# Four half pieces of expert 0's weights: the subtraction of the split on VectorE instead of GpSimd, in units 16 to 19

## The chip, the cores and the metric

The kernel runs on one core of a Trainium2 chip. The metric is the device time of one execution in microseconds (us). An engine runs its own instructions in the order in which they were written; engines wait for each other by semaphores.

## The reference

Local and global attention, then a mixture of experts (MoE), in float32. Eight batches of eight heads hold 512 local and 32 global positions of width 64; a local query sees the global keys and the local ones at most 32 positions away:

```python
out_g = softmax(scale * q_g @ k_all.T) @ v_all
out_l = softmax(concat(scale * q_l @ k_g.T, where(|i - j| <= 32, scale * q_l @ k_l.T, -1e9))) @ concat(v_g, v_l)
x = concat(out_g, out_l) as rows of 512               # 4608 tokens
keep = x @ w_skip > 0
e = argmax(x[keep] @ w_gate)                          # one of 8 experts
out[keep] = x[keep] + gate * relu(x[keep] @ w1[e]) @ w2[e]
```

The MoE multiplies with weights and activations that are each split into a high and a low part: `hi` is the value cast to the matmul type float32r, and `lo = value - hi`. Three matmuls (hi by hi, hi by lo, lo by hi) stand for one.

## The kernel before

**Attention** runs in 32 units, numbered u. A unit is two heads of one batch, four units a batch. It is a software pipeline of three: in iteration u the names `cur`, `prev` and `old` are units u, u-1 and u-2. The list `ORDER` (L758) gives the order of the steps in an iteration, and with manual scheduling this is the order of each engine's queue. The steps that matter here:

- `cur.scores 0/1` (TensorE, L380) and `cur.probs 0` to `probs 3` (L393, L398): for each two windows VectorE adds the mask and finds the extreme, and ScalarE takes the exponential with its sum. The first such VectorE instruction of a unit reads the mask `m_first`; it marks the unit's start below. There are six of eight window instructions ahead of the step `split_mid`, the last two (`probs 3`) behind it.
- `cur.normal 0/1` (VectorE, L430, L431) invert the sums; `cur.scale 0/1` (GpSimd, L435) multiply the probabilities by them. `prev.turn_g 0/1` (VectorE, L511) read what they leave.
- `prev.scale_g` (GpSimd, L468), in odd iterations only, scales the global queries' probabilities; `prev.turn_pg` (TensorE, L492, L493) transposes them and `prev.turned_pg` (ScalarE L501, VectorE L504) copies them out.
- `old.gather_g 0`, `old.leave 0` (VectorE, L567, L560), `cur.window_min` (VectorE, L420, even units), `cur.probs_g` (VectorE L452, ScalarE L457, even units), `prev.turned 0` (VectorE, L483).
- `sends` (GpSimd, L691): two indirect DMAs a unit that write finished rows of the expert lists to DRAM. They stand ahead of `cur.scale 1` in GpSimd's queue.

**The split of expert 0's weights** is done during attention. Eight pieces of 128x1024 are loaded ahead, and each is split in two halves of 128x512, one half a unit from unit 4 to unit 19. A half is a cast on ScalarE (L188) that writes the high part, and a subtraction (L189) that reads the loaded piece and that high part, both in SBUF, and writes the low part. Up to unit 16 the step is `split`, the last of the iteration; from unit 17 it is `split_mid`, between `prev.scale_g` and `old.values 1`. The result is first read by the MoE, after the 32 units. Later experts' weights are split on VectorE, whole pieces at a time, through the same function.

**The MoE** runs the eight experts one after the other, with the next expert's weights loaded and split meanwhile.

Of the kernel before, what the change touches and what calls it, by code (L numbers as in the profile page):

```python
# [44 lines left out]
def kernel(  # L45
# [12 lines left out]
    nc = tc.nc  # L58
# [42 lines left out]
    def index(es, g):  # L101
        nc.vector.tensor_copy(six[:, es, g], lt[:, es, g, :, 0])
# [14 lines left out]
    def gather(xg, gidx, nrow=NT):  # L117
        for t in range(NSUB):
            ins = nc.gpsimd.indirect_dma_start(  # L119
                out=xg[:, t, :], out_offset=None, in_=out[0:nrow, :],  # L120
                in_offset=bass.IndirectOffsetOnAxis(ap=gidx[:, t:t + 1], axis=0),
                bounds_check=nrow - 1, oob_is_err=False,
            )
            apart(ins, "gathers", "scatters")
# [3 lines left out]
    def tick(n=1):  # L128
        for _ in range(n):
            if stages:  # L130
                stages.pop(0)()

    def send_some(n):
        for _ in range(n):
            if sends:
                sends.pop(0)()
# [54 lines left out]
    weights = {0: Weights(0, w1a, v1a, w2a)}  # L191
# [9 lines left out]
    def turn_x(xg, i, nt=NSUB):  # L201
        xh, xl = xs[i]
        for t in range(nt):
            pt = ps_t("xt")
            for c in range(NC):
                nc.tensor.transpose(  # L206
                    pt[:, c * P:(c + 1) * P], xg[:, t, c * P:(c + 1) * P], ident
                )
            p3 = pt.rearrange("p (c n) -> p c n", n=P)
            ts_ = slice(t * P, (t + 1) * P)  # L210
            step = NC if nt > 1 else NC // 2
            for c in range(0, NC, step):
                nc.scalar.copy(xh[:, c:c + step, ts_], p3[:, c:c + step])  # L213
            nc.vector.tensor_sub(xl[:, :, ts_], p3, xh[:, :, ts_].bitcast(F32))  # L214
        return xh, xl
# [4 lines left out]
    with ExitStack() as actx:  # L220
# [55 lines left out]
        def consts_pool():  # L276
            nc.gpsimd.memset(xfirst, 0.0)
            nc.gpsimd.affine_select(
                out=tri, in_=ones, pattern=[[1, P]], compare_op=ALU.is_gt,
                fill=0.0, base=0, channel_multiplier=-1,  # L280
            )
            nc.gpsimd.iota(ids_i, pattern=[[S, B], [P, 5]], base=SG, channel_multiplier=1)
            for hf in range(2):
                for bb in range(4):
                    nc.gpsimd.iota(
                        ids_i[bb * 32:(bb + 1) * 32, 4 * hf + 3, 4:5], pattern=[[0, 1]],
                        base=(4 * hf + bb) * S, channel_multiplier=1,
                    )
            nc.gpsimd.iota(tmp[:, 0, :], pattern=[[-1, E]], base=E, channel_multiplier=0)
            nc.gpsimd.iota(tmp[:, 1, :], pattern=[[CAP, E]], base=0, channel_multiplier=0)  # L290
# [25 lines left out]
        def load_qg(b):  # L316
            for h in range(2):
                hp = slice(h * D, (h + 1) * D)
                nc.sync.dma_start(
                    qgs[b % 2][hp, :, h * 32:(h + 1) * 32],  # L320
                    qgT[b, :, hp, :].rearrange("p d q -> d p q"),
                )

        def load_vg(b):

            for h in range(2):
                for o in range(2):
                    r = (2 * h + o) * 32
                    nc.sync.dma_start(
                        vgs[b % 2][r:r + 32, :, o, :], vgl[b].rearrange("p s d -> s p d")  # L330
                    )

        def load_pair(u):
            b, p = divmod(u, NP)
            nc.sync.dma_start(ks[u % NQ].rearrange("d r o m -> d (r o m)"), kT[b, p])
            n = SL // 2 if u == 0 else SL
            for i in range(0, SL, n):
                nc.sync.dma_start(qs[u % NQ][:, i:i + n], qT[b, p, :, i:i + n])

        def load_v(u):  # L340
            b, p = divmod(u, NP)
            nc.sync.dma_start(vw[u % NV].rearrange("k i d -> k (i d)"), v[b, p])
# [430 lines left out]
        with tc.manual_schedule(engines=engines):  # L773
# [19 lines left out]
            for u in range(NU + 2):  # L793
                cur = pair(u) if u < NU else None

                nth = iter(range(8))

                def seam():
                    tick(1 if u < NU - 4 else 2)
                    if u >= NU or u == NU - 2 and next(nth) in (0, 1, 4, 5):  # L800
                        send_some(1)

                def late_rows():
                    for b, k in LATE_ROWS.get(u, ()):
                        batch_rows(b, k)
                    if u == NU - 1:
                        for k in range(5):
                            batch_rows(B - 1, k, (0,))

                def loads_g():  # L810
                    if u < NU and u % NP == 2 and u // NP + 1 < B:
                        load_qg(u // NP + 1)
                        load_vg(u // NP + 1)

                def loads_pair():
                    if u + 2 < NU:
                        load_pair(u + 2)

                def loads_v():
                    if 2 <= u + 1 < NU:  # L820
                        load_v(u + 1)

                def early_rows():
                    bp, kp = divmod(u - 6, NP)
                    if 0 <= bp < B - 3:
                        batch_rows(bp, kp)
                        if kp == 3 and bp % 4 == 3:
                            batch_rows(bp, 4)

                def first_x():  # L830
                    if u == NU - 1:
                        index(first, 0)
                        gather(xfirst, six[:, 0, 0, :], (B - 2) * S)

                def last_x():
                    if u == NU:
                        x2.append(turn_x(xfirst, 0))

                def setup():
                    if u == 0:  # L840
                        consts_pool()

                def setup_late():
                    if u == 1:
                        clear_batch(1)
                        consts_late()

                def split():
                    if u == NU - 1:
                        for _ in range(2):  # L850
                            load_piece(1)
                    if u == 3:
                        weights[0].load()
                    if 4 <= u <= 16:
                        split_one()

                def split_mid():
                    if u > 16:
                        split_one()

                def split_one():
                    if u % 2 == 0:
                        weights[0].load()
                    weights[0].split(nc.gpsimd, 2)

                def after():
                    if u == NU - 2:
                        send_some(len(sends))
                        slots(first, 0)
                    if u == NU - 1:  # L870
                        tick(len(stages))

                def last_sends():
                    if u == NU - 1:
                        send_some(len(sends))

                def some_sends():
                    if u < NU - 1:
                        send_some(2 if u < NU - 3 else 4)

                loose = dict(
                    loads_g=loads_g, loads_pair=loads_pair, loads_v=loads_v,
                    rows=early_rows, late_rows=late_rows, first_x=first_x, setup=setup,
                    setup_late=setup_late, split=split, after=after, seam=seam, sends=some_sends,
                    last_sends=last_sends, split_mid=split_mid, last_x=last_x,
                )
                for step in ORDER:
                    name, _, arg = step.partition(" ")
                    if name in loose:
                        loose[name]()  # L890
                        continue
                    who, name = name.split(".")
                    it = dict(cur=cur, prev=prev, old=old)[who]
                    if it is None or name in PAIR and it.u % 2:
                        continue
                    getattr(it, name)(*([int(arg)] if arg else []))
                prev, old = cur, prev
# [269 lines left out]
```

## Time and profile before

| | |
|---|---|
| median of 3 runs | 474.61 us (474.32, 474.61, 477.75) |
| the profiled execution | 478.56 us, of which its span (first to last instruction) is 476.8 us |
| busy over the span | TensorE 92%, VectorE 64%, ScalarE 60%, GpSimd 49% |
| attention, the last unit's start | 202.85 us |
| the 16 subtractions of expert 0's split | GpSimd, 35.1 to 125.4 us, 20.4 us in all |

In the rows below PE is TensorE, PEld its weight load, DVE VectorE, ACT ScalarE, POOL GpSimd. Times are us from the span's start, unless a column says ns. The shares of the whole span average attention and MoE, which have different limits, so the rows are taken from the units that the change touches. A timeline row is: start, duration, engine, line, operation, output<-inputs with shapes, count, and in brackets the engine's idle time before it with what ended it.

### The profile page before, as it was taken

How to read it: one execution, taken by the hardware profiler on the slowest of the kernel's cores; microseconds unless marked ns; L12 is line 12 of the kernel's file. 1: busy time of each engine (PE TensorE's matmuls, PEld its weight loads, DVE VectorE, ACT ScalarE, POOL GpSimd, SP SyncE). 2: the span in 40 equal slices, each digit the busy share in tenths (PEclk: the TensorE clock that was granted, in tenths of full speed). 3: DMA queues.
4: the chain of work that ended last, by engine and by line, in shares of the span. 5: the costliest groups of instructions: out<-in, count | busy, mean ns of one | idle time of the engine just before them, and what ended most of it. 6: DMA issues, size and time to landing. Idle time of an engine off the chain costs nothing. (4 is left out here: it accounts for less than half of the span.)

```text
span 476.8 us, 13622 instructions
## 1 busy us (share of the span) xinstructions
PE 438.9 (92%) x4962; PEld 370.8 (78%) x4962; DVE 307.1 (64%) x1239; ACT 283.8 (60%) x867; POOL 231.9 (49%) x238
## 2 busy tenths in 40 slices
PE   7799999998899999788979999999999999899991
PEld 3687878786788776667958898979879898698980
DVE  7798888997779889864533184848417574166510
ACT  5599999998889998664412072728126272254500
POOL 7557777789966878873442050505005150032300
PEclk9799999999999999999989999999999999999996
DMA  7998898989898896412637047575604858037000
GB/s 250 301 346 282 282 312 310 316 286 305 248 314 256 218 294 155 128 46 90 112 60 284 24 143 281 164 267 172 256 1 136 309 153 305 3 104 257 27 18 17
DMA packets 50593, 93.32 MB, mean 196 GB/s; under 512 B 15644, under 2 KB 19996, under 8 KB 50496
## 3 DMA queue, kind: packets, MB, share of 16 engines
q1 hardware_dynamic: 44384, 80.78, 53.1%
q0 software_dynamic: 6112, 11.30, 7.1%
q8 instruction: 55, 0.90, 0.8%
q14 instruction: 42, 0.34, 0.3%
HBM read 82.91 MB, written 14.67 MB: 205 GB/s over the span
## 5 line engine op out<-in xcount | busy, mean ns | idle before, releaser
L398 ACT ACTIVATE prob<-prob,nmx 128x160 f32<-128x160 f32 x256 | 106.7, 423 | 16.4 <-DVE nmx L393 16.1
L435 POOL TENSOR_TENSOR prob<-prob,inv 128x640 f32<-128x640 f32 x64 | 80.5, 1260 | 33.8 <-DVE inv L431 15.0
L1008 POOL DMA_INDIRECT out_dram<-yo,six x12 | 12.2, 1016 | 125.4 <-DVE yo L1007 107.9
L931 ACT ACTIVATE hh<-ph 128x256 fp32r<-128x256 f32 x72 | 27.7, 384 | 66.3 <-PE ph L926 60.4
L942 PE MATMUL py<-w2h,hh 128*128 128x512 f32 x144 | 57.0, 396 | 0.0
L942 PE MATMUL py<-w2h,hlw 128*128 128x512 f32 x144 | 56.4, 391 | 0.0
L942 PE MATMUL py<-w2l,hh 128*128 128x512 f32 x144 | 56.3, 391 | 0.0
L380 PE MATMUL pss<-ks,qs 64*64 64x160 f32 x1024 | 52.5, 309 | 3.5 <-DMA qs<-in_qT_dram 1.7
L532 PEld LDWEIGHTS pv<-ptT,vw 128*64 128x64 f32 x1024 | 41.4, 138 | 18.4 <-issue 9.9
L398 ACT ACTIVATION_READ_ACCUMULATOR prob<-prob,nmx 128x1 f32 x256 | 49.4, 193 | 0.0
L532 PE MATMUL pv<-ptT,vw 128*64 128x64 f32 (+1 forms) x1024 | 47.8, 240 | 0.8 <-DVE ptT L483 0.2
L926 PE MATMUL ph<-xh,w1h 128*128 128x256 f32 x288 | 46.0, 282 | 2.3 <-DVE xl L214 1.1
L926 PE MATMUL ph<-xh,w1l 128*128 128x256 f32 x288 | 45.3, 279 | 0.0
L926 PE MATMUL ph<-xl,w1h 128*128 128x256 f32 x288 | 45.3, 279 | 0.0
L380 PEld LDWEIGHTS pss<-ks,qs 64*64 64x64 f32 x1024 | 35.3, 135 | 11.3 <-issue 7.3
L932 DVE SCALAR_TENSOR_TENSOR hlw<-ph,hh 128x256 fp32r<-128x256 f32 x72 | 30.0, 418 | 20.2 <-ACT hh L931 19.4
L213 ACT CAST xh<-xt 128x512 fp32r<-128x512 f32 (+1 forms) x22 | 11.2, 550 | 52.9 <-PE xt L206 52.9
L926 PEld LDWEIGHTS ph<-xh,w1h 128*128 128x128 f32 x288 | 38.8, 188 | 4.7 <-issue 3.2
L691 POOL DMA_INDIRECT lst<-dat,slu x34 | 34.6, 1017 | 15.0 <-issue 6.3
L476 PE MATMUL pst<-ident,prob 128*128 128x128 f32 x256 | 39.7, 281 | 0.0
L926 PEld LDWEIGHTS ph<-xl,w1h 128*128 128x128 f32 x288 | 38.9, 189 | 0.0
L926 PEld LDWEIGHTS ph<-xh,w1l 128*128 128x128 f32 x288 | 38.7, 188 | 0.0
(179 smaller groups left out, 972.8 us busy)
## 6 DMA issues: line engine op xcount, KB each, us to landing
raw<-in_w_dram SPq DMA_DIRECT2D x58, 512.0 KB, 6.6
vw<-in_v_dram SPq DMA_DIRECT2D x32, 512.0 KB, 6.3
ks<-in_kT_dram SPq DMA_DIRECT2D x32, 400.0 KB, 5.1
out_dram<-xr SPq DMA_DIRECT2D x32, 256.0 KB, 4.5
qs<-in_qT_dram SPq DMA_DIRECT2D x31, 256.0 KB, 4.9
raw<-in_w_dram POOLq DMA_DIRECT2D x6, 512.0 KB, 8.0
vgs<-in_vgl_dram SPq DMA_DIRECT2D x32, 64.0 KB, 5.4
lst<-dat,slu POOLq DMA_INDIRECT x34, 4.5
```

The lines of the kernel that those rows point to most:

```text
L213: nc.scalar.copy(xh[:, c:c + step, ts_], p3[:, c:c + step])
L380: nc.tensor.matmul(banks[odd][head(h ^ odd), j * W:(j + 1) * W], q[head(h), w * QB:(w + 1) * QB], window(k[head(h)], w), start=True, stop= ...
L398: nc.scalar.activation(pt[:, i, :], pt[:, i, :], AF.Exp, bias=nmx[:, i:i + 1], scale=-1.0, accum_out=sums[:, i, 0:1],)
L435: nc.gpsimd.tensor_mul(pt[:, sl, :], pt[:, sl, :], inv[:, sl].unsqueeze(2).to_broadcast([P, 4, W]),)
L476: nc.tensor.transpose(pst[:, i * P:(i + 1) * P], pt[:, 4 * hf + i, 0:KW], ident)
L532: nc.tensor.matmul(pv[head(h), j * 96:j * 96 + n], vv[:, w, head(h)], ptT[:, w, h ^ odd, 0:n], start=False, stop=j == 3, skip_group_check= ...
L691: ins = nc.gpsimd.indirect_dma_start(out=lst, out_offset=bass.IndirectOffsetOnAxis(ap=slu[:, t:t + 1], axis=0), in_=dat[:, bs[j], t - 4 * ...
L926: nc.tensor.matmul(ph[:, 0:GRP], hl[a][:, c, f * P:(f + 1) * P], bb[:, c, :], start=i == 0, stop=i == 3 * NC - 1,)
L931: nc.scalar.activation(hh[:, f, :], ph[:, 0:GRP], AF.Relu)
L932: nc.vector.scalar_tensor_tensor(hlw[:, f, :], ph[:, 0:GRP], 0.0, hh[:, f, :].bitcast(F32), ALU.max, ALU.subtract,)
L942: nc.tensor.matmul(py, a[:, f, ts_], hl[bb][:, f, :], start=f == 0 and i == 0, stop=f == NF - 1 and i == 2,)
L1008: ins = nc.gpsimd.indirect_dma_start(out=out, out_offset=bass.IndirectOffsetOnAxis(ap=sidx, axis=0), in_=yo, in_offset=None, bounds_check= ...
```

## The change

The first sixteen halves were subtracted by GpSimd. Now the halves of units 4 to 15 still are, and those of units 16, 17, 18 and 19 go to VectorE. The place in the order of steps, the casts on ScalarE and the loads are the same.

```diff
                 def split_one():
                     if u % 2 == 0:
                         weights[0].load()
-                    weights[0].split(nc.gpsimd, 2)
+                    weights[0].split(nc.gpsimd if u < 16 else nc.vector, 2)
```

`Weights.split` (L182), which it calls, is unchanged:

```python
                nc.scalar.copy(hi, raw)
                eng.tensor_sub(lo, raw, hi.bitcast(F32))
```

## Rows read from the trace of the kernel before

**Rows 1.** First line of the profile page.

```profile
span 476.8 us, 13622 instructions
```

**Rows 2.** Stages: units 17 to 20, cut at each unit's first m_first instruction.

```profile
core 0: us, PE busy (x) PEld busy (x) DVE busy (x) ACT busy (x) POOL busy (x), PEclk, DMA share, GB/s
106.57:114.47 7.90, 6.42 (x131) 5.55 (x121) 5.23 (x32) 6.85 (x26) 7.42 (x8) 1.00 1.03 305
114.47:120.80 6.33, 6.33 (x112) 4.38 (x108) 5.26 (x32) 5.94 (x23) 5.76 (x6) 1.00 1.14 303
120.80:128.15 7.35, 5.57 (x117) 4.85 (x109) 4.81 (x30) 6.19 (x24) 6.86 (x7) 1.00 0.70 190
128.15:133.71 5.56, 5.56 (x111) 4.46 (x104) 5.01 (x32) 5.11 (x21) 4.92 (x5) 1.00 1.00 348
```

**Rows 3.** Waits, 106.4 to 128 us: waiter <- releaser: total us, times, longest.

```profile
PE psgT L492 <- POOL probg L468: 3.3, 2, 1.8
DVE pgT L511 <- POOL prob L435: 2.4, 5, 0.5
```

**Rows 4.** Groups by line: forms, count | busy us, mean ns.

```profile
L189 DVE TENSOR_TENSOR w2l<-raw,w2h 128x1024 fp32r<-128x1024 f32 x28 | 34.1, 1217 | 3.6 <-ACT w2h L188 3.6
...
L214 DVE TENSOR_TENSOR xl<-xt,xh 128x512 fp32r<-128x512 f32 x20 | 13.2, 687 | 22.9 <-ACT xh L213 22.9
...
L189 POOL TENSOR_TENSOR w2l<-raw,w2h 128x512 fp32r<-128x512 f32 x8 | 10.2, 1281 | 0.2
```

**Rows 5.** Timeline of VectorE, units 16 to 20.

```profile
106.35 0.30 DVE L511 STREAM_TRANSPOSE pgT<-prob 128x128 f32<-128x128 f32 x1
...
108.38 0.29 DVE L567 TENSOR_REDUCE xTg<-pv 128x32 f32<-128x128 f32 x1
...
115.91 0.22 DVE L420 CUSTOM_DVE_ANT_1 smg<-pss,zero 128x64 f32<-128x64 f32 x1
...
116.94 0.29 DVE L393 CUSTOM_DVE_ANT_0 prob<-pss,m_odd 128x160 f32<-128x160 f32 x1
...
122.48 0.28 DVE L567 TENSOR_REDUCE xTg<-pv 128x32 f32<-128x128 f32 x1
...
131.65 0.31 DVE L511 STREAM_TRANSPOSE pgT<-prob 128x128 f32<-128x128 f32 x1 [0.48 <-POOL prob L435]
```

**Rows 6.** Timeline of ScalarE, units 16 to 19.

```profile
106.64 0.61 ACT L188 CAST w2h<-raw 128x512 fp32r<-128x512 f32 x1
...
107.62 0.44 ACT L398 ACTIVATE prob<-prob,nmx 128x160 f32<-128x160 f32 x1
...
110.11 0.61 ACT L188 CAST w2h<-raw 128x512 fp32r<-128x512 f32 x1
...
118.12 0.43 ACT L398 ACTIVATE prob<-prob,nmx 128x160 f32<-128x160 f32 x1
...
121.19 0.43 ACT L398 ACTIVATE prob<-prob,nmx 128x160 f32<-128x160 f32 x1
```

**Rows 7.** Timeline of GpSimd, end of unit 16.

```profile
107.07 0.98 POOL L691 DMA_INDIRECT lst<-dat,slu  x1 [0.30 <-DVE nmx L393]
108.06 1.28 POOL L435 TENSOR_TENSOR prob<-prob,inv 128x640 f32<-128x640 f32 x1
```

**Rows 8.** One line's instructions: count: ns min/median/max, first and last start.

```profile
L671 DVE TENSOR_TENSOR oh<-mx,first x5: 202/873/1833, 92.4 to 225.1; 128x64 f32<-128x64 f32 x2, 128x72 f32<-128x72 f32 x1, 128x32 f32<-128x32 f32 x1, 128x40 f32<-128x40 f32 x1
```

**Rows 9.** Timeline of both engines, 143.9 to 145.3 us.

```profile
143.94 1.25 POOL L435 TENSOR_TENSOR prob<-prob,inv 128x640 f32<-128x640 f32 x1 [1.65 <-DVE inv L431]
...
144.41 0.87 DVE L671 TENSOR_TENSOR oh<-mx,first 128x72 f32<-128x72 f32 x1
```

**Rows 10.** Timeline of both engines, 198.4 to 200.3 us.

```profile
198.46 1.83 DVE L671 TENSOR_TENSOR oh<-mx,first 128x32 f32<-128x32 f32 x1
...
198.97 1.27 POOL L435 TENSOR_TENSOR prob<-prob,inv 128x640 f32<-128x640 f32 x1
```

## The prediction

> **What bounds the kernel now.** I forecast against the profiled execution, 478.56 us with a span of 476.8 us [rows 1]. The three runs have their median at 474.61 us, 4.0 us lower, so I work out a difference in us and add it to the median. Changes below 1% (4.7 us) can't be told from no change here.
>
> The first view is the table of stages, cut where a unit starts, at its first VectorE instruction on the scores [rows 2]. The whole-span shares on the page put GpSimd at half busy, which is an average with the MoE, where it does little. In unit 17 it is busy 7.42 of 7.90 us, in unit 18 5.76 of 6.33, in unit 19 6.86 of 7.35: over 90% each time, while VectorE is busy 5.23, 5.26 and 4.81 us. Unit 20, without a subtraction, has GpSimd at 4.92 of 5.56 us. So three of the four changed places lie where GpSimd sets the pace.
>
> The second view, the waits in these units, says the same from the other side [rows 3]: TensorE waits 3.3 us, twice, for the scaled global probabilities, and VectorE 2.4 us, five times, for the scaled ones. Read so, the change takes work off the bound. What the two views don't show is where a subtraction on VectorE would have to stand, and that decides my forecast.
>
> **What is removed.** Four instructions of 1.28 us on GpSimd [rows 4], 5.1 us in all. All of it is on the path of units 17 to 19 at most; I count the gain not by itself but in the unit lengths below, which are worked out as if GpSimd were never late.
>
> **What is added: four subtractions on VectorE.** This form, 128x512 with both inputs in SBUF, isn't in the trace. The same line with 1024 columns takes 1.217 us, and a 512-column subtraction with one input in PSUM 0.687 us [rows 4]. I take 0.69 us, the row of the same size; its bounds are half the long one, 0.61 us, and the whole long one, 1.22 us. The casts on ScalarE, the loads and SP's queue keep their places; the four loaded pieces come free at about the same time, and nothing else asks for their buffers before the last unit.
>
> **What is moved: a wait for ScalarE into the middle of VectorE's queue.** The subtraction needs the cast ahead of it. GpSimd came to its subtractions long after the casts; VectorE runs ahead of ScalarE and comes too early. Everything behind it on VectorE, which also feeds ScalarE's next exponentials, waits with it.
>
> *Unit 16.* The cast runs from 106.64 to 107.25 [rows 6]. In VectorE's queue the subtraction stands right ahead of the transpose that started at 106.35 [rows 5]. Starting 0.03 after the cast and taking 0.69 us, it ends at 107.97. Unit 17 therefore starts later by 107.97 - 106.35 = **1.62 us**.
>
> *The cast within a unit.* The first exponential comes 0.39 us after the unit's start when ScalarE isn't behind (unit 19: 121.19 against 120.80 [rows 2, 6]). Six exponentials stand ahead of the cast and took 110.11 - 107.62 = 2.49 us in unit 17; the cast takes 0.61 [rows 6]. So its result is there 0.39 + 2.49 + 0.61 = 3.49 us after the unit's start. VectorE reaches that place after its six score instructions: in unit 17 at 108.38 - 106.57 = 1.81 us, in unit 18 at 115.91 - 114.47 = 1.44 us, in unit 19 at 122.48 - 120.80 = 1.68 us [rows 2, 5]. The forced idle times are 1.68, 2.05 and 1.81 us.
>
> *Unit 17.* VectorE's own work 5.23, the subtraction 0.69 and the idle time 1.68 make 7.60 us against 7.90: **-0.30 us**. The GpSimd waits that it had are gone, and the new wait takes their place almost exactly.
>
> *Unit 18.* 5.26 + 0.69 + 2.05 = 8.00 us against 6.33: **+1.67 us**. VectorE's idle time before was 6.33 - 5.26 = 1.07 us, all that GpSimd's lateness can have cost here.
>
> *Unit 19.* ScalarE starts it somewhat late. In unit 18 the subtraction ends at 3.49 + 0.69 = 4.18 us; from L420 to the next score instruction VectorE needs 116.94 - 115.91 = 1.03 us [rows 5], and I add 0.37 until ScalarE has its result (the 0.39 above less one hop): 5.58. From there to the next unit's first exponential ScalarE needs 121.19 - 118.12 = 3.07 us without a pause [rows 6], so 8.65 us after unit 18's start, which is 0.65 after unit 19's instead of 0.39. The idle time is then 1.81 + 0.26 = 2.07 us, and the unit 4.81 + 0.69 + 2.07 = 7.57 us against 7.35: **+0.22 us**.
>
> *Unit 20.* GpSimd's backlog is gone, so the wait of 0.48 us at 131.65 [rows 5] disappears: **-0.48 us**.
>
> The sum is 1.62 - 0.30 + 1.67 + 0.22 - 0.48 = **+2.7 us**. Attention goes on in the same order, and the MoE begins when its last lists are written, so I carry the whole of it to the end: 474.61 + 2.7 = **477.3 us**, 0.6% slower. With the subtraction at 0.61 us the sum is 0.3 us less, at 1.22 us 2.1 us more (4 x 0.53).
>
> **Two engines at SBUF.** VectorE's L671 takes two SBUF inputs and 0.20 us at its shortest, but 1.83 at its longest [rows 8]. At 144.41 it took 0.87 us: GpSimd's multiplication had begun at 143.94 and ended at 145.19, and L671 ended 0.09 after that [rows 9]. So such a VectorE instruction waits for a multiplication of GpSimd that is under way. In units 17 to 19 as I have laid them out, GpSimd has finished or not begun one when the subtraction is issued, within 0.2 us in unit 19. In unit 16 the subtraction is issued at 107.28 and would end at 107.97, before the multiplication of 108.06 [rows 7].
>
> The Trainium skill, "SBUF — State Buffer", section "Who interferes with whom", says that a VectorE instruction with two SBUF inputs contends with a GpSimd instruction that reads SBUF, and that whoever issues first has the shared port for the whole instruction. The trace agrees where GpSimd was first (held to 0.09 us past the multiplication's end [rows 9]). By that rule unit 16's subtraction, issued first, is not held, and the sum stays +2.7 us.
>
> Another row points the other way: at 198.46 L671 began 0.51 us *before* the multiplication of 198.97, should have been done in 0.20 us, and yet ended at 200.29, 0.05 us after that multiplication's end at 200.24 [rows 8, 10]. Unit 16 has the same order, a send and then the multiplication [rows 7].
>
> **The rivals.**
> - *Held in unit 16.* The subtraction behaves as at 198.46 and waits for the end of the multiplication, 108.06 + 1.28 = 109.34. It starts 109.34 - 107.28 = 2.06 us later, with everything behind it: +4.8 us, 479.4 us. For it speaks the one row with the same order; against it that its start was 0.51 us ahead of the multiplication, here 0.78 us. Chance 0.30.
> - *Relief wins* (the other side). VectorE doesn't lose time at the casts, because ScalarE, also freed of its waits, brings them before VectorE needs them. Then the waits of rows 3 go, 3.3 + 2.4 us, and 4 x 0.69 us is paid: -2.9 us, 471.7 us. It decides for this where the cast's result is there less than about 1.7 us after the unit's start; six exponentials alone need 2.49. Chance 0.10.
> - *Absorbed.* The loss is there in unit 20 and is made up by waits in the twelve units behind, 0 us, 474.6 us. Nothing in rows 2 shows a resource with an own timetable; a transfer could be one. Chance 0.12.
> - *Forecast as summed*, 0.48.
>
> **How the numbers follow.** The likeliest case gives 477.3 us; its own range, with 0.61 to 1.22 us for the subtraction, is 477.0 to 479.4. The range 474.0 to 480.4 takes in the absorbed case, with 0.6 us for the runs' own spread below it, and the held one with 1 us for a longer subtraction, and leaves out the relief case. Slower by over 1% (above 479.4): half of the held case, 0.15, and 0.07 of the likeliest with a long subtraction, 0.22. Faster by over 1% (below 469.9): only a relief beyond its price, 0.03. The rest, 0.75, is within 1%.
>
> **What would show it.** Right: in units 16 to 19 VectorE has a wait for the cast (L188) ahead of L189, near 0.9, 1.7, 2.0 and 2.1 us, with L189 at 0.69 us each; ScalarE idles 1 us or more ahead of the last two exponentials of units 17 to 19; unit 18 takes about 8.0 us and the others about what they did; GpSimd drops below 85% and nobody waits for it. A first L189 of 2.7 us instead of 0.69 is the held case. Wrong: unit 20 starting no later than before, or units 21 to 31 getting shorter than they were by more than half a us in all.

## The result: 0.55% slower, and the profile after

The changed kernel takes 478.15 us in the median of 21 runs, the kernel before 475.66 us in 21 runs beside it. The ratio is 1.0055, with a 95% interval of [1.0039, 1.0071], so the change costs 2.6 us (1.9 to 3.4). The forecast was +2.7 us. (The two profiled executions, 478.57 us after and 478.56 before, don't show it: they are single ones. Between the start of unit 15 and the start of unit 31 they differ by 110.85 - 107.49 = 3.4 us; unit 16 begins at 101.20 us before and 100.10 after, and the MoE differs again behind. I therefore compare lengths of units.)

Units 17 to 20 after the change, in the columns of [rows 2]:

```profile
107.58:114.91 7.33, 5.33 (x71) 4.43 (x71) 5.44 (x33) 5.41 (x22) 4.39 (x4) 0.85 1.04 284
114.91:122.53 7.62, 7.62 (x128) 5.49 (x124) 5.65 (x32) 6.00 (x22) 4.62 (x5) 0.92 0.94 233
122.53:130.37 7.84, 6.33 (x118) 4.95 (x111) 5.24 (x32) 6.32 (x25) 5.59 (x6) 1.00 0.93 312
130.37:135.78 5.41, 5.41 (x100) 4.41 (x104) 5.10 (x32) 5.28 (x21) 4.04 (x5) 1.00 0.82 157
```

Against [rows 2], unit 17 is 0.57 us shorter, unit 18 1.29 longer, unit 19 0.49 longer, unit 20 0.15 shorter. GpSimd is busy for 4.39 of 7.33 us, 4.62 of 7.62 and 5.59 of 7.84: it no longer sets the pace, and still the four units together are 1.06 us longer, behind a unit 16 that is 2.11 us longer (7.48 against 5.37). The waits between 106.4 and 130 us, in the columns of [rows 3], say what does:

```profile
POOL prob L435 <- DVE inv L431: 6.8, 3, 2.5
DVE w2l L189 <- ACT w2h L188: 6.2, 4, 2.2
ACT prob L398 <- DVE nmx L393: 4.9, 4, 1.5
...
PE psgT L492 <- POOL probg L468: 1.2, 2, 0.7
```

VectorE, for which the old profile had no wait on ScalarE's cast, now waits for it four times, 6.2 us. Two waits follow from it: ScalarE waits for VectorE's masked scores (L393), 4.9 us, and GpSimd for the inverted sums (L431), 6.8 us. GpSimd, which the others waited for, now mostly waits itself. TensorE's wait for it fell from 3.3 us [rows 3] to 1.2, and VectorE's 2.4 us are gone. In VectorE's timeline, in order, the transpose that starts late (compare 106.35 in [rows 5]) stands right behind the first subtraction:

```profile
106.74 0.69 DVE L189 TENSOR_TENSOR w2l<-raw,w2h 128x512 fp32r<-128x512 f32 x1 [0.85 <-ACT w2h L188]
107.35 0.30 DVE L511 STREAM_TRANSPOSE pgT<-prob 128x128 f32<-128x128 f32 x1
...
111.09 0.69 DVE L189 TENSOR_TENSOR w2l<-raw,w2h 128x512 fp32r<-128x512 f32 x1 [1.74 <-ACT w2h L188]
...
116.54 0.33 DVE L393 CUSTOM_DVE_ANT_0 prob<-pss,m_even 128x160 f32<-128x160 f32 x1 [0.57 <-PE pss L380]
...
118.45 0.69 DVE L189 TENSOR_TENSOR w2l<-raw,w2h 128x512 fp32r<-128x512 f32 x1 [1.33 <-ACT w2h L188]
...
126.55 0.69 DVE L189 TENSOR_TENSOR w2l<-raw,w2h 128x512 fp32r<-128x512 f32 x1 [2.24 <-ACT w2h L188]
```

All four take 0.69 us. ScalarE, ahead of the last two exponentials of units 17 and 18 (unit 19's, at 128.31, waited 1.52 us):

```profile
112.85 0.43 ACT L398 ACTIVATE prob<-prob,nmx 128x160 f32<-128x160 f32 x1 [1.53 <-DVE nmx L393]
...
120.36 0.43 ACT L398 ACTIVATE prob<-prob,nmx 128x160 f32<-128x160 f32 x1 [1.10 <-DVE nmx L393]
```

So ScalarE makes VectorE wait for a cast, and then stands idle, because what it needs next is queued on VectorE behind the subtraction. GpSimd at the end of unit 16, answering to [rows 7]:

```profile
106.47 0.98 POOL L691 DMA_INDIRECT lst<-dat,slu  x1 [0.30 <-issue]
107.45 1.29 POOL L435 TENSOR_TENSOR prob<-prob,inv 128x640 f32<-128x640 f32 x1
```

The first subtraction (106.74 to 107.43) ran through the send at its full speed and was done before the multiplication. It was not held.

### The profile page after: what moved, and what is told of

It is laid out like the page before. It is cut to its first block, busy times and chain, and to the rows that moved or that the text cites. A ratio compares the mean times of both kernels' runs of the same rounds, so it can differ in the third digit from the quotient of the medians.

```text
span 476.8 us, 13627 instructions
## 1 busy us (share of the span) xinstructions
PE 441.6 (93%) x4962; PEld 371.9 (78%) x4962; DVE 308.8 (65%) x1243; ACT 284.4 (60%) x867; POOL 227.4 (48%) x234
## 5 line engine op out<-in xcount | busy, mean ns | idle before, releaser
L380 PE MATMUL pss<-ks,qs 64*64 64x160 f32 x1024 | 54.5, 314 | 2.3 <-DVE nmx L393 1.8
L380 PEld LDWEIGHTS pss<-ks,qs 64*64 64x64 f32 x1024 | 36.6, 138 | 11.6 <-issue 6.3
L189 DVE TENSOR_TENSOR w2l<-raw,w2h 128x1024 fp32r<-128x1024 f32 (+1 forms) x32 | 36.9, 1154 | 9.7 <-ACT w2h L188 9.7
```

Source lines behind the costliest of these rows:

```text
L189: eng.tensor_sub(lo, raw, hi.bitcast(F32))
L380: nc.tensor.matmul(banks[odd][head(h ^ odd), j * W:(j + 1) * W], q[head(h), w * QB:(w + 1) * QB], window(k[head(h)], w), start=True, stop= ...
```

## The experiments

For every kernel I cut attention at each unit's first m_first instruction. All times are us; the sum is of units 16 to 21. Units 8 to 15 agree between the kernels within about 0.02 us, and units 22 to 30 within 0.05, apart from what is named below. A *stall* is here a unit that is longer in one execution than in others with the same instructions in it, for no cause that the profile shows. The code cuts are shortened to what differs. The kernel before, profiled and timed once more under a label of its own (e8), repeats its sum within 0.1 us. From the last unit's start to the end of the span it took 474.2 - 201.88 = 272.3 us, and the first profile 476.8 - 202.85 = 273.9: single executions of one kernel differ by 1.6 us behind attention, so their whole times can't show the change.

> The kernel before, as a run of its own. Every theory expects a ratio of 1.000 and the unit lengths of before within 0.05 us; what it differs by is the error of these comparisons, and its profile shows whether the stretch behind attention, with its granted clock, differs from one execution to the next by 1 us or more.

| kernel | 16 | 17 | 18 | 19 | 20 | 21 | sum | timed, ratio to before |
|---|---|---|---|---|---|---|---|---|
| before | 5.37 | 7.90 | 6.33 | 7.35 | 5.56 | 7.35 | 39.86 | |
| before again (e8) | 5.38 | 7.91 | 6.33 | 7.36 | 5.57 | 7.36 | 39.91 | 0.9980 [0.9948, 1.0012] |
| **the change** | 7.48 | 7.33 | 7.62 | 7.84 | 5.41 | 7.50 | 43.18 | 1.0055 [1.0039, 1.0071] |
| only unit 16 (e1) | 6.93 | 6.31 | 6.33 | 7.36 | 5.57 | 7.36 | 39.86 | 1.0032 [1.0006, 1.0058] |
| only 17 to 19 (e2) | 5.80 | 8.95 | 7.63 | 7.83 | 5.41 | 7.51 | 43.13 | 1.0054 [1.0015, 1.0094] |
| later on VectorE (e3) | 5.73 | 7.99 | 6.50 | 6.05 | 5.19 | 7.51 | 38.97 | 0.9965 [0.9942, 0.9988] |
| the wait alone (e4) | 6.39 | 6.88 | 7.05 | 7.30 | 5.42 | 7.50 | 40.54 | 1.0007 [0.9983, 1.0032] |
| later still (e5) | 5.37 | 7.35 | 6.25 | 7.47 | 5.20 | 7.51 | 39.15 | 0.9958 [0.9924, 0.9992] |
| GpSimd, later units (e6) | 5.37 | 6.38 | 6.38 | 7.72 | 5.43 | 7.51 | 38.79 | 0.9955 [0.9919, 0.9992] |
| e5, work twice (e7) | 5.52 | 8.75 | 6.97 | 6.49 | 5.19 | 7.51 | 40.43 | 1.0000 [0.9971, 1.0029] |
| wait and relief (e9) | 6.38 | 6.79 | 7.06 | 7.29 | 5.41 | 7.51 | 40.44 | one execution: 478.38 us beside 476.87 |
| wait and work, no relief (e10) | 6.93 | 7.33 | 7.59 | 7.84 | 5.41 | 7.51 | 42.61 | one execution: 480.39 us beside 476.87 |
| GpSimd, later odd units (e11) | 5.38 | 6.38 | 6.37 | 5.84 | 5.40 | 7.50 | 36.87 | 0.9955 [0.9927, 0.9983] |
| e6 again (e12) | 6.05 | 6.34 | 8.07 | 5.74 | 6.03 | 7.50 | 39.73 | one execution: 483.98 us beside 482.00 |

### The two parts of the change: unit 16 (e1) and units 17 to 19 (e2)

Both edits are shown against the line of the change:

```diff
-  weights[0].split(nc.gpsimd if u < 16 else nc.vector, 2)
+  weights[0].split(nc.vector if u == 16 else nc.gpsimd, 2)    # e1
+  weights[0].split(nc.vector if u > 16 else nc.gpsimd, 2)     # e2
```

> Only unit 16's subtraction is on VectorE; units 17 to 19 stay on GpSimd. Theory 'wait' (VectorE stands still for the cast, and GpSimd's relief gives part back): unit 17 starts about 1.6 us later than in the kernel before, but GpSimd, still the bound of units 17 to 19 and relieved of one 1.2 us piece, makes up about 1.2 us of it; in the end +0.3 to +0.5 us. Rival 'work' (VectorE pays for its own 0.69 us each, wherever it stands): +0.7 us. Rival 'additive' (each of my terms holds by itself): +1.6 us.

> Units 17 to 19 on VectorE, unit 16 on GpSimd as before. Theory 'wait': unit 16 as before, units 17 to 19 about 22.4 to 23 us in all instead of 21.6 us, since GpSimd still carries one piece ahead of unit 17: in the end +2 to +3 us, most of the whole change. Rival 'work': 3 x 0.69 = +2.1 us. Rival 'additive': 2.7 - 1.6 = +1.1 us.

Moving unit 16's subtraction lengthens that unit by 6.93 - 5.37 = 1.56 us, as forecast, but unit 17 gives back 1.59: without the subtraction in its queue, GpSimd comes to unit 17 with no backlog. The sum is unchanged. With e2, which is as long as the whole change (43.13 and 43.18), this says that the cost lies in units 17 to 19. The change's unit 16 is 0.55 us longer than e1's with the same edit; TensorE's queue stands without a visible releaser near 100.3 us of that execution, so I count it as that execution's and not the change's. Unit 16 is longer in e2 (5.80 us), e3 (5.73) and e12 (6.05) too, none of which adds work there. e1's timed +0.32% doesn't fit its equal trace. The kernel before, timed against itself (e8), came out at 0.998, so differences of 0.3% between sets of runs are not safely one kernel's. e2's units 17 to 19 take 24.41 us where 22.4 to 23 were expected; 0.83 us of that is the hold that follows, the rest is not explained.

In e2 the first subtraction began 0.32 us after one of GpSimd's multiplications had begun, and was held. The timeline of both engines in e2:

```profile
110.56 1.27 POOL L468 TENSOR_TENSOR probg<-probg,ing 128x640 f32<-128x640 f32 x1
...
110.88 1.52 DVE L189 TENSOR_TENSOR w2l<-raw,w2h 128x512 fp32r<-128x512 f32 x1 [2.41 <-ACT w2h L188]
```

Its last 0.69 us begin at 111.71, when the multiplication (to 111.83) was all but over.

### The same work later in the unit (e3, e5), and twice the work (e7)

```diff
-  eng.tensor_sub(lo, raw, hi.bitcast(F32))
+  late_subs.append(lambda: eng.tensor_sub(...))       # u >= 16, on VectorE
...
-  "cur.probs 3", "rows",
+  "cur.probs 3", "sub_late", "rows",                  # e3
-  "prev.turned_pg", "cur.normal 1",
+  "prev.turned_pg", "sub_late", "cur.normal 1",       # e5; e7 runs each one twice there
```

`sub_late` runs what is in the list, so unit 16's half, which is cast at the end of that unit, falls into unit 17 with unit 17's own: two together, then one, then one.

> All four subtractions on VectorE as in the change, the casts at their old places, but each subtraction moved behind the last two score instructions (probs 3) of its unit, that of unit 16 to the same place of unit 17, so that its cast is long done. Theory 'wait': no wait of 0.5 us or more ahead of L189; VectorE's extra 4 x 0.69 us is hidden and GpSimd's relief remains: 1 to 1.5 us faster than the kernel before, 3.5 to 4 us faster than the change. Rival 'work': as slow as the change, +2.6 us, since the same work is on the same engine.

> As the run with the subtractions behind probs 3 (e3_late), which was held four times by GpSimd's multiplications (L189 of 1.0 to 2.7 us instead of 0.69), but the four subtractions now stand ahead of the step cur.normal 1, where GpSimd is at its sends. Theory 'wait': no wait for a cast, L189 at 0.69 us each, units 16 to 20 in all 1 to 2 us shorter than in the kernel before: -1 to -2 us. Rival 'work': +2.6 us as the change. Rival 'held' (a send followed by a multiplication holds VectorE, as one row of the kernel before suggests): L189 of 1.5 us or more here, and no gain over e3_late.

> As e5_ahead_normal1 with each of the four subtractions done twice on VectorE, 4 x 0.6 us more work at the same place (the second writes the same values). Theory 'wait': VectorE has idle time there, at most half of the 2.4 us shows: 0 to +1.2 us against e5_ahead_normal1. Rival 'work': +2.4 to +2.8 us against it.

VectorE does the same four subtractions, in the same units but for that one, and units 16 to 21 take 38.97 and 39.15 us: 0.9 and 0.7 less than before, and 4 less than in the change. The timing says 0.9965 [0.9942, 0.9988] and 0.9958 [0.9924, 0.9992]. So the work on VectorE is not what costs by itself; the place is. VectorE's line in e5, with no wait ahead of any of them:

```profile
110.69 1.30 DVE L190 TENSOR_TENSOR w2l<-raw,w2h 128x512 fp32r<-128x512 f32 x2
...
117.56 0.69 DVE L190 TENSOR_TENSOR w2l<-raw,w2h 128x512 fp32r<-128x512 f32 x1
...
125.04 0.68 DVE L190 TENSOR_TENSOR w2l<-raw,w2h 128x512 fp32r<-128x512 f32 x1
```

e5's unit 19 has a stall of its own: TensorE stood there for 2.02 us with no releaser shown; e3's and e7's unit 19, without one, are 1.0 to 1.4 us shorter. With it e5 gained 0.9 us in units 16 to 20, where 1 to 2 were expected.

In e3 the cast is not long done in units 18 and 19: almost half a us of waiting for it is left, and GpSimd's multiplications hold the subtraction besides.

```profile
117.23 1.01 DVE L190 TENSOR_TENSOR w2l<-raw,w2h 128x512 fp32r<-128x512 f32 x1 [0.49 <-ACT w2h L188]
...
123.72 1.04 DVE L190 TENSOR_TENSOR w2l<-raw,w2h 128x512 fp32r<-128x512 f32 x1 [0.46 <-ACT w2h L188]
```

The first of e3's pair in unit 17 ran under two multiplications and took 2.08 us (of that below), the second 0.68: three of the four were held, and not all four, as the expectation for e5 has it.

Doubling the work (e7) adds 1.3 us to e5's sum, but the stall in e5's unit 19 hides the rest. In units 17 and 18 neither has one, and there two more subtractions add 1.40 us and one more adds 0.72. That is their whole length, as the rival "work" has it for e7, and not the half that I expected. The timed ratio says the same, with 1.0000 [0.9971, 1.0029] after 0.9958, which is 2.0 us. So the room on VectorE is small: one subtraction costs nothing in unit 18 (6.25 us in e5, and 6.37 without any in e11 below), two cost 0.97 us in unit 17 (7.35 against 6.38), and any more cost all of their time.

### The wait alone (e4), with the relief (e9), and with the work (e10)

```diff
   nc.scalar.copy(hi, raw)
+  nc.vector.tensor_copy(seen, hi[:, 0:1].bitcast(F32))   # e4, e9: u >= 16, 128x1
+  nc.vector.tensor_sub(lo, raw, hi.bitcast(F32))         # e10: u >= 16, beside GpSimd's
   eng.tensor_sub(lo, raw, hi.bitcast(F32))               # on GpSimd; e9: in units 21, 23, 25, 27
```

The copy of one column waits for the same cast in the same place, and takes 0.15 us. e4 leaves all work on GpSimd; e9 takes it off GpSimd in these units as well (as e11 does, below); e10 subtracts on both engines, so that GpSimd gets no relief.

> All subtractions stay on GpSimd as before; at the four places of the change VectorE copies one column of the cast's result into a scratch tile, about 0.1 us, and so waits for the cast without taking work from GpSimd. Theory 'wait': VectorE waits 0.85 us or more ahead of each copy, ScalarE idles ahead of its last two exponentials as in the change; but GpSimd's pace hides part of it in units 17 and 19: in the end +1 to +2 us. Rival 'work': 4 x 0.1 us, +0.4 us at most.

> The waits of the change without its work on VectorE, and with GpSimd relieved: at the four places VectorE copies one column of the cast's result (about 0.1 us), and GpSimd's four subtractions are put off to the ends of units 21, 23, 25 and 27. Read from the lengths of units 16 to 21, which repeat within 0.1 us (39.86 us before, 43.18 in the change, 40.54 with the copies alone). Theory 'exposed work' (the wait makes VectorE's queue the pace of the unit, and each subtraction that stands behind it adds its full 0.6 us; GpSimd's pace is then covered): 40.3 to 41.0 us, as with the copies alone. Rival 'sum of parts' (wait +0.7, relief -1.1): 39.5 us.

> Wait and work on VectorE without relief: the four subtractions are done by VectorE at the places of the change and then once more by GpSimd as before (the same values). Units 16 to 21: theory 'exposed work': 43 to 43.8 us, as in the change, since GpSimd is not the bound once VectorE waits. Rival 'sum of parts' (the change plus the 1.1 us of relief given back): 44.3 us or more.

The waits of e4:

```profile
DVE seen L191 <- ACT w2h L189: 6.8, 4, 2.2
ACT prob L401 <- DVE nmx L396: 3.3, 4, 1.1
PE psgT L495 <- POOL probg L471: 2.2, 2, 1.5
```

and the first three of e9:

```profile
DVE seen L191 <- ACT w2h L189: 6.8, 4, 2.2
POOL prob L443 <- DVE inv L439: 6.0, 4, 2.0
ACT prob L406 <- DVE nmx L401: 3.3, 4, 1.1
```

A copy of 0.15 us makes VectorE wait as long as the real subtraction does. In e4 that costs only 0.7 us in the trace and nothing that the timing can tell, against an expected 1 to 2 us: TensorE still waits 2.2 us for GpSimd, against 3.3 before [rows 3], so most of the old wait is still there and the new one lies beside it. With GpSimd relieved (e9) nothing is gained over e4, 40.44 against 40.54, as expected of "exposed work" (40.3 to 41.0), and the rival's 39.5 is false: once VectorE waits, taking work off GpSimd is worth 0.1 us. GpSimd's 6.0 us of waiting for VectorE in e9 shows where it went. The work behind the wait (e10 over e4) is 42.61 - 40.54 = 2.1 us. The subtraction is 0.69 - 0.15 = 0.54 us longer than the copy, four times 2.2, so all of it shows; over e9, e10's units 16 to 19 are 0.55, 0.54, 0.53 and 0.55 us longer. e10's four lines are those of the change, within 0.2 us:

```profile
106.76 0.69 DVE L190 TENSOR_TENSOR w2l<-raw,w2h 128x512 fp32r<-128x512 f32 x1 [0.85 <-ACT w2h L188]
111.12 0.69 DVE L190 TENSOR_TENSOR w2l<-raw,w2h 128x512 fp32r<-128x512 f32 x1 [1.74 <-ACT w2h L188]
118.44 0.69 DVE L190 TENSOR_TENSOR w2l<-raw,w2h 128x512 fp32r<-128x512 f32 x1 [1.51 <-ACT w2h L188]
126.54 0.69 DVE L190 TENSOR_TENSOR w2l<-raw,w2h 128x512 fp32r<-128x512 f32 x1 [2.25 <-ACT w2h L188]
```

In e10 GpSimd has more to bear than in e4: its subtraction writes the tile that VectorE has just written, and waits for that, three times, 2.4 us. Even so the sum is the change's without its stall (43.18 - 0.55 = 42.63). The 43 to 43.8 that I expected had the stall in it; the rival's 44.3 or more is false. Once VectorE's queue sets the pace, GpSimd's load in these units no longer matters.

### The relief alone: the work stays on GpSimd, later (e6, e11, e12)

```diff
-  "last_sends", "split",
+  "last_sends", "split", "sub_late",     # the last step, on GpSimd
...
+  if late_subs and u > 20: late_subs.pop(0)()                 # e6, e12: units 21 to 24
+  if late_subs and u > 20 and u % 2: late_subs.pop(0)()       # e11: units 21, 23, 25, 27
```

> All subtractions on GpSimd; those of units 16 to 19 are put off to the ends of units 21 to 24, where GpSimd has idle time, the casts stay. This is GpSimd's relief alone, with no work and no wait on VectorE. Theory 'wait': units 16 to 20 take about 2 to 2.5 us less in all than in the kernel before, units 21 to 25 the same: -2 to -2.5 us. If it is 0, GpSimd was not the bound of these units and the table of stages was misread.

> The kernel of e6_gpsimd_later once more, one look. Up to the end of unit 21 it issues the same instructions in the same order as e11_odd_units, yet its units 16 to 21 took 38.79 us against 36.87, nearly all of it in unit 19 (7.72 against 5.84), where ScalarE stood 1.8 us ahead of a copy whose input was there. If that belongs to the kernel, unit 19 takes 7.7 us again, and GpSimd's relief alone is worth 1.1 us; if it is a chance stall of that one execution, unit 19 takes about 5.8 us, units 16 to 21 about 36.9 us, and the relief is worth 3.0 us.

> GpSimd keeps all subtractions; the four are put off to the ends of the odd units 21, 23, 25 and 27. Put off to units 21 to 24 they gained 1.1 us in units 16 to 21 and lost 1.0 and 1.2 us in units 23 and 25, each behind an even unit's end, where GpSimd's scale_g comes next. All theories: units 16 to 21 38.8 us (-1.1 us). If scale_g's lateness was the cause of the loss, units 22 to 25 keep the lengths of before within 0.2 us and the whole is 0.7 to 1.1 us faster than before; if any subtraction in these units costs, 1 us or more is lost again.

e6 gained 1.1 us in units 16 to 21 where 2 to 2.5 were expected. Its unit 19 took 7.72 us, with this line in it:

```profile
123.67 0.37 ACT L565 COPY xT<-pv 128x256 f32<-128x256 f32 x1 [1.80 <-PE pst L481]
```

The same kernel once more (e12) has 5.74 us there, and e11 5.84: the stall was that execution's. (e12's sum is not the 36.9 us expected: it has stalls of its own in units 16, 18 and 20, and later ones in 27 and 29.) e6 also loses 1.0 us in unit 23 and 1.2 in unit 25, each behind a subtraction at the end of an even unit, where `prev.scale_g` comes next in GpSimd's queue. e11 avoids those ends. Units 17 to 20 of e11, in the columns of [rows 2]:

```profile
105.47:111.85 6.38, 6.14 (x120) 5.32 (x115) 5.23 (x32) 6.38 (x26) 5.88 (x6) 1.00 0.99 295
111.85:118.22 6.37, 6.37 (x104) 4.36 (x104) 5.19 (x31) 6.27 (x23) 5.27 (x5) 1.00 1.06 223
118.22:124.06 5.84, 5.80 (x125) 5.05 (x121) 4.77 (x30) 5.84 (x25) 5.22 (x6) 1.00 0.94 255
124.06:129.46 5.40, 5.40 (x100) 4.40 (x104) 5.10 (x32) 5.26 (x21) 3.52 (x4) 1.00 1.08 318
```

That is what taking the subtractions off GpSimd is worth when nothing else is put in the way: 39.86 - 36.87 = 3.0 us in units 16 to 21, with ScalarE now busy for the whole of units 17 and 19 and TensorE for the whole of unit 18. It is more than one execution's luck: e6 repeats units 16 to 18 within 0.01 us, and e12 units 17 and 19 within 0.1. The waits of [rows 3] added up to 5.7; by these rows the gain ends where ScalarE or TensorE has hardly any idle time left. e11 (and e9 likewise) gives 1.9 us back in units 28 and 29 (8.28 and 8.75 us against 6.71 and 8.46), behind the subtraction at the end of unit 27, an odd one, so that the lateness of `prev.scale_g` is not the only thing that a late subtraction can cost. At 0.9955 [0.9927, 0.9983] it is timed below the kernel before, as e3, e5 and e6 are. With e1's 0.32% in mind I take from this that none of the four is slower; their intervals overlap, so none is shown to be the best.

## Why the prediction was right, step by step

**GpSimd sets the pace of units 17 to 19.** Right for 17 and 19: its work gone, with no wait added, the three shrink by 1.52, -0.04 and 1.51 us (e11). Wrong for unit 18, which [rows 2] show with TensorE busy for all of its 6.33 us: the prediction read GpSimd's 91% there as the bound. Nor did GpSimd come to all its subtractions long after the casts, as the prediction has it: in unit 18 it began 0.08 us after the cast's end. (The forecast doesn't rest on either, since it works out the units as if GpSimd were never late.)

```profile
117.35 0.60 ACT L188 CAST w2h<-raw 128x512 fp32r<-128x512 f32 x1
...
118.03 1.29 POOL L189 TENSOR_TENSOR w2l<-raw,w2h 128x512 fp32r<-128x512 f32 x1
```

**VectorE comes too early and waits for the cast.** Right in each place. Forecast 0.9, 1.7, 2.0 and 2.1 us; found 0.85, 1.74, 1.33 and 2.24. In unit 18 VectorE had already waited 0.57 us for scores, which makes 1.90; e4, without that wait, has 2.00 for the cast. That this wait is the cause is shown from both sides: the same work with little of it (e3) or none (e5) takes less than before, and the wait without the work, GpSimd relieved, lifts 36.87 (e11) to 40.44 (e9), +3.6 us. It acts in two ways: it eats up the relief, and it makes VectorE's queue the pace, so that the subtraction behind it shows in full.

**The subtraction takes 0.69 us and isn't held in unit 16.** Right, in e1 and e10 too, and the rival at 479.4 us is false: 0.69 us, done before the multiplication began.

**The sum.** Added up one part at a time, from the kernel before by way of e11 and e9 to the change: the relief -3.0 us (e11), the four waits +3.6 (e9), the work behind them +2.7 (the change over e9, of which 0.55 is the stall in unit 16, so about 2.2). That leaves +2.8 without the stall, +3.3 with it, and the timing says +2.6 (1.9 to 3.4). The way by e4 and e10 gives the same: the wait +0.7, the work +2.1, the relief then nothing. The forecast of +2.7 came from terms of which some were off:

| term | forecast | found |
|---|---|---|
| unit 16 | +1.62 | +1.56 (e1); +2.11 in the change, stall included |
| unit 17 | -0.30 | -0.57 |
| unit 18 | +1.67 | +1.29 |
| unit 19 | +0.22 | +0.49 |
| units 20 and 21 | -0.48 | -0.15 and +0.15 |

The mis-sized pieces: I took VectorE's own work to be as long as before. Without the subtraction it is 5.44 - 0.69 = 4.75 us in unit 17, 4.96 in unit 18 and 4.55 in unit 19, which is 0.48, 0.30 and 0.26 less than in [rows 2]. Behind the subtraction its queue now runs with no pause (in unit 18 from 119.06 to the next unit's start at 122.53), and queued instructions overlap a little in the record (the one at 119.06 takes 0.22 us, the next begins at 119.20); that this is the whole reason is not shown. It made units 17 and 18 too high. Unit 19 was too low, since it has a second wait that I had not seen, 0.26 us for an exponential (L430 at 129.28), and a wait for the cast of 2.24 instead of 2.07. Unit 20's gain was counted although unit 21 takes it back. The terms found add up to +2.8 us; that they come so near to +2.7 is partly luck, since four of the five missed by 0.27 us or more.

**The rivals.** *Relief wins* is false by its own condition: it needed the cast within 1.7 us of the unit's start, and the casts end 3.48 (unit 17: 110.46 + 0.60 - 107.58), 3.51 and 3.99 us after it. *Absorbed* is false: units 22 to 30 have the lengths that they had, and the loss reaches the end of attention whole. "GpSimd drops below 85%" and "ScalarE idles 1 us or more" came as forecast: 60%, 61% and 71%, and 1.53, 1.10 and 1.52 us. That nobody waits for GpSimd did not quite: TensorE still does, 1.2 us in two waits.

**Where I was wrong in the experiments.** I expected the wait alone to cost 1 to 2 us (e4: 0.7, not told apart by the timing), since I had not seen that it lies beside GpSimd's lateness, I expected less from the relief than the 3.0 us that e11 shows, and I expected VectorE to hide at least half of a second subtraction (e7), of which it hides nothing.

Open: why e1 was timed 0.32% slower with an equal sum; what the stalls of some 0.4 to 2.3 us in single units of single executions are; why the subtraction at the end of unit 27 costs and those of 21, 23 and 25 don't; whether e11 without the subtraction in unit 27 keeps the 1.9 us (not tried).

## What to carry to other kernels

Before moving an instruction to an engine with idle time, look where in that engine's queue it will stand, and whether its input is there by then: an engine that runs ahead of its producer turns idle time into a wait for everything queued behind. Here the same four subtractions on the same engine made units 16 to 21 take 43.2 us beside the cast (39.9 before; timed 0.55% slower) and 39.2 later in the unit (timed 0.08 to 0.76% faster, e5). Behind such a wait the work shows in full, 0.55 us for each 0.54, even on an engine that was idle for a sixth to a third of these units. And count a relief only up to the next engine: the 5.7 us of waits on GpSimd were worth 3.0, and 0.1 once VectorE waited instead.

## What the runs showed of the hardware

**In e3 a VectorE instruction was held through two multiplications of GpSimd.** In e3 VectorE's first subtraction began while a multiplication of GpSimd ran, and another stood behind that. The timeline of both engines in e3:

```profile
108.37 1.27 POOL L473 TENSOR_TENSOR probg<-probg,ing 128x640 f32<-128x640 f32 x1
...
109.33 2.08 DVE L190 TENSOR_TENSOR w2l<-raw,w2h 128x512 fp32r<-128x512 f32 x1
...
109.58 1.27 POOL L440 TENSOR_TENSOR prob<-prob,inv 128x640 f32<-128x640 f32 x1
```

It took 2.08 us instead of 0.69. So it was held for 1.39, until 110.72, which is 0.13 us before the end of the *second* multiplication, and that one began 0.25 us after VectorE's instruction. The Trainium skill, "SBUF — State Buffer", section "Who interferes with whom", gives the shared port to whoever issues first, for the whole instruction. The trace agrees for a single multiplication: in e2, and in e3's units 18 and 19 (1.01 and 1.04 us), the last 0.69 us begin 0.12, 0.14 and 0.15 us before its end ([rows 9] are alike). For the second one here it doesn't, by the starts in the trace. The 1.83 us of [rows 8, 10] may be of this kind, but there only one multiplication follows, and the changed kernel has it again:

```profile
200.71 1.85 DVE L671 TENSOR_TENSOR oh<-mx,first 128x32 f32<-128x32 f32 x1
```

It begins 0.50 us ahead of the multiplication at 201.21, inside a send, while the change's first subtraction ran through a send in 0.69. What tells them apart stays open.

**TensorE's clock fell after the new wait.** In unit 17 of the change TensorE's queue stood for 1.48 us, until 112.46, for sums that VectorE had yet to add up (L493 for L430), and its granted clock then went from 1.00 to 0.50, the lower of its two levels (1.2 of 2.4 GHz). In slices of 1 us, in the columns of [rows 2]:

```profile
110.00:111.00 1.00, 0.65 (x4) 0.42 (x4) 0.00 (x0) 1.00 (x6) 0.27 (x1) 1.00 1.11 346
111.00:112.00 1.00, 0.00 (x0) 0.00 (x0) 0.91 (x3) 0.32 (x2) 0.00 (x0) 1.00 0.98 207
112.00:113.00 1.00, 0.54 (x4) 0.57 (x5) 0.97 (x8) 0.15 (x1) 0.23 (x1) 0.83 1.03 273
113.00:114.00 1.00, 1.00 (x11) 0.65 (x13) 0.93 (x7) 1.00 (x5) 1.00 (x1) 0.50 1.34 313
114.00:115.00 1.00, 1.00 (x24) 0.94 (x20) 0.99 (x4) 1.00 (x4) 0.85 (x2) 0.50 0.83 144
115.00:116.00 1.00, 1.00 (x24) 0.98 (x20) 0.97 (x8) 0.95 (x4) 0.69 (x2) 0.50 0.84 312
116.00:117.00 1.00, 1.00 (x26) 0.76 (x23) 0.46 (x3) 1.00 (x7) 0.99 (x2) 0.96 1.05 392
```

The matmuls from 113 to 116 us ran at the lower level, and VectorE's 0.57 us wait for scores at 116.54 is the trace of it. It cost little, because VectorE would have waited until the cast anyway: its wait in unit 18 ends 3.54 us after the unit's start, and 3.52 in e9, which has no dip. e2 and e10 show the same dip (0.86 and 0.89 in unit 17), e3, e4, e5 and e9 none.
